# Start-up of a fused convolution and two-layer kernel: one small load on another queue, the first chunk's convolution cut by tokens, copies and w_out slots in another order

## The chip, the cores and the metric

The kernel runs on one core of a Trainium2 chip. Its time is device microseconds for one execution. Before the change, three executions took 680.83, 681.26 and 681.55 us, a median of 681.26 us. The engines are named as the profile names them: PE (TensorE matmuls), PEld (its weight loads), DVE (VectorE), ACT (ScalarE), POOL (GpSimd), SP (SyncE). SPq, ACTq and POOLq are their sequencers, which issue DMAs.

## The reference, cut to what matters

`x` is 8 x 4096 x 192 (batch, sequence, features), `weight` 8 x 7, `moe_w_in` 192 x 2048, `moe_w_out` 2048 x 192, all fp32. The output is 32768 x 192 fp32.

```python
w = exp(weight - max(weight)); w = w / (sum(w) + 1e-9)      # 8 heads x 7 taps
x_pad = 6 zero rows ahead of each sequence
y[b, s, head, :] = sum over k of w[head, k] * x_pad[b, s + k, head, :]   # 24 features a head
h = y.reshape(32768, 192) @ w_in
g = maximum(0.01 * h, h)
out = g @ w_out
```

So there are a causal convolution with seven taps, a matrix product to 2048 features, a leaky ReLU and a product back to 192.

## The kernel before, in words

**Layout.** Two sequences are worked on at a time: one in partitions 0 to 63, one in 64 to 127 (`e` = 0 and 1), and the 192 features are three chunks of 64 (`c`). So `xt` and `yt` hold features on partitions and tokens along a row. The tokens are cut into blocks of 512. A *group* (L72) is a block, except that the first two blocks are halved: groups with index 0 to 3 have T = 256 tokens (times two sequences), from index 4 on T = 512.

**The pipeline.** For each group, `mm1` (L488) multiplies `yt` with `w_in` for step `u` into the PSUM tile `ph` (two buffers), and ACT applies the leaky ReLU from `ph` into `g` (L515). For T = 256 a group has eight steps `u`, 12 matmuls each; for T = 512 sixteen steps. A loop index `j` holds two steps. The second product comes a group later in *slots*: up to index 4, `mm2_row_slot` (L533) issues two matmuls of 64x192 a slot (L525), after that `mm2_slot` (L568). How many slots follow which `j` is written out by hand in `plan` (L650); `between` (L656) says how many of them are put ahead of each of the two steps of a `j`. Sixteen slots make a round, and between the two rounds of a pair PE waits for a small ACT instruction (L555).

**The convolution.** From index 2 on it runs on DVE, as 21 taps a group (L222, L228), issued during the group before. For indices 0 and 1 most of it runs on PE: `pe_conv_jobs` (L244) multiplies `xt` with diagonal 64x64 matrices `diag` (part 0 the bf16 taps, part 1 their remainders, seven taps each) into PSUM, and an evacuation scales by `rsum` (L268). With `cross=True` each half's output goes to the opposite half of the PSUM partitions, so that two such lists, run together, use all four 64x64 quarters of the array. Group 1's chunk 1 is convolved on DVE (`conv_1`, L690) while its chunks 0 and 2 are on PE, cut into three stretches by `CUTS` (L53): after `u` = 1, 3 and 5 of group 0. Their evacuation follows `u` = 5 (L703).

**The order of the start.** Instructions go to each engine in the order of the program text (the schedule is manual), and each engine runs its own in order.

- SP issues x's first 256 tokens as two DMAs (L142); ACT issues the taps' DMA `w9` (L288), then loads its function table (L366) and computes the exponentials (L372). DVE splits them into bf16 parts `w9p` (L379 to L382).
- PE runs `warm` matmuls (L360), then `select` (L396) spreads the taps over partitions into `wps`. ACT casts x's first half (L155) and half of the second; DVE casts the rest (L155), *then* copies the taps (L409) and makes the six parts of `diag` (L420).
- PE transposes x (L181), ACT copies it to `xt` (L195), PE convolves group 0 (L259).
- `w_in` comes by POOL DMAs in bf16. Half of its rows stand in the wrong partitions for one of the sequences: `spread_up` (L326) and `spread_down` (L322) copy them across. The first half of `w_in` (`w_in[0]`) is copied in a *near* and a *far* part of 512 columns, the second (`w_in[1]`), which step `u` = 4 reads first, after that.
- Chunk 0 of group 0 is convolved as 28 matmuls of 256 columns: the bf16 part into one PSUM tile (`hi`), the remainders, crossed, into another. ACT scales the remainders into `low` (L455, two instructions), and DVE joins both to `yt` (L465). Chunks 1 and 2 follow as 56 matmuls of 256 columns.

Of the kernel before, what the change touches and what calls it, by code (L numbers as in the profile page):

```python
# [10 lines left out]
FP32 = mybir.dt.float32  # L11
# [4 lines left out]
def kernel(  # L16
# [8 lines left out]
    nc = tc.nc  # L25

    B, S, D = x.shape
    H, K = weight.shape
# [11 lines left out]
    HT = ST // 2  # L40
# [9 lines left out]
    for k in range(K):  # L50
        SKEW += [(2, k), next(pair)]
    SKEW += [(1, 5), (0, 6), (1, 6)]
    CUTS = {1: (0, 6), 3: (6, 11), 5: (11, 14)}  # L53
    GB = 32
    NR = D // (2 * GB)

    const_pool = ctx.enter_context(tc.tile_pool(name="const", bufs=1))
# [14 lines left out]
    groups = [(b, h * HT, HT) for b in range(NHALF) for h in range(2)]  # L72
# [162 lines left out]
    def y_of(grp, c):  # L235
        blk, t0, T = grp
        if blk not in yt:
            yt[blk] = yt_pool.tile([128, NCH, ST], BF16, name="yt")
        return yt[blk][:, c, t0 : t0 + T]

    def acc_tile():
        return psum_o.tile([128, ST], FP32, name="acc", tag="po")

    def pe_conv_jobs(grp, c, cross=False, parts=range(2), accs=None):  # L244

        blk, t0, T = grp
        accs = accs or [acc_tile()] * 2
        jobs = []  # L250
        for p in parts:
            for k in range(K):
                a = BASE + k + blk * ST + t0
                both = []
                for e in range(2):
                    ps = slice(e * CH, (e + 1) * CH)
                    to = slice((e ^ cross) * CH, ((e ^ cross) + 1) * CH)
                    both.append(
                        lambda k=k, p=p, a=a, ps=ps, to=to, acc=accs[e]: nc.tensor.matmul(  # L259
                            out=acc[to, :T], lhsT=diag[c][ps, p, k, :],  # L260
                            rhs=xt[0][ps, c, a : a + T],
                            start=(k == 0 and p == parts[0]),
                            stop=(k == K - 1 and p == parts[-1]),
                        )
                    )
                jobs.append(both)

        def evac(*scale, out=None):  # L268
            out = y_of(grp, c) if out is None else out
            if not cross:  # L270
                scale[0](out, accs[0][:, :T], rsum[:, c, :])
                return
            for e in range(2):
                ps = slice(e * CH, (e + 1) * CH)
                frm = slice((1 - e) * CH, (2 - e) * CH)
                scale[e](out[ps], accs[e][frm, :T], rsum[frm, c, :])

        return jobs, evac

    def run(*lists):  # L280
        for slots in zip_longest(*lists, fillvalue=()):
            for both in slots:
                for job in both:
                    job()


    w9 = const_pool.tile([H, K + 1], FP32, name="w9")
    nc.scalar.dma_start(out=w9[:, 0:K], in_=weight)  # L288
    load_first(0)

    ones = nc.const_aps.tensor(1.0, [128, ST], BF16)
# [7 lines left out]
    for sign, off in ((1, 0), (-1, GRP - 1)):  # L299
        nc.gpsimd.affine_select(  # L300
            out=sel[:, :, 0, :], in_=sel[:, :, 0, :], compare_op=mybir.AluOpType.is_ge,
# [10 lines left out]
    near, far = slice(0, WF // 2), slice(WF // 2, WF)  # L312
# [8 lines left out]
    def spread_down(n, copy=nc.vector.tensor_copy, cols=slice(0, WF)):  # L321
        copy(out=w_in[n][0:CH, 1, cols], in_=w_in[n][CH:128, 0, cols])  # L322

    def spread_up(n, slots=slice(0, 3, 2), cols=slice(0, WF)):
        to = slice(slots.start // 2 + 1, (slots.stop - 1) // 2 + 2)
        nc.vector.tensor_copy(out=w_in[n][CH:128, to, cols], in_=w_in[n][0:CH, slots, cols])  # L326
# [21 lines left out]
    for h in range(2):  # L348
        cs = slice(h * NFC // (2 * RUN), (h + 1) * NFC // (2 * RUN))
        nc.gpsimd.dma_start(  # L350
            out=w_out.rearrange("p (c i) d -> p c i d", i=RUN)[:, cs],
            in_=moe_w_out.rearrange("(c p i) d -> p c i d", p=128, i=RUN)[:, cs],
# [5 lines left out]
    def warm(n, cols=HT, to=wa[:, 0]):  # L358
# [10 lines left out]
        out=nmax, in_=w9[:, 0:K], axis=mybir.AxisListType.X,  # L369
# [3 lines left out]
        out=w9[:, 0:K], in_=w9[:, 0:K], func=mybir.ActivationFunctionType.Exp,  # L373
# [18 lines left out]
    def select(out, parts):  # L392
# [17 lines left out]
        out=taps, in_=wps_hm[..., None].to_broadcast([128, NCH, 2, K + 1, 2])  # L410
# [5 lines left out]
    def diag_wide(c, p):  # L416
# [16 lines left out]
    rsum = const_pool.tile([128, NCH, 1], FP32)  # L433
# [5 lines left out]
        out=rsum, in0=wml[:, :, K:], scalar=1e-9, in1=taps[:, :, 0, K:, 0],  # L439
        op0=mybir.AluOpType.add, op1=mybir.AluOpType.add,  # L440
# [7 lines left out]
    load_x(2)  # L448
    diag_wide(1, 1)
    diag_wide(2, 1)  # L450
    spread_up(0, slice(0, 1), near)
    spread_down(0, cols=near)

    def act_scale(out, in_, scale):
        nc.scalar.activation(  # L455
            out=out, in_=in_, func=mybir.ActivationFunctionType.Copy, scale=scale
        )

    hi = acc_tile()
    low = const_pool.tile([128, HT], FP32, name="low")  # L460
    pe_hi, _ = pe_conv_jobs(groups[0], 0, parts=(0,), accs=[hi] * 2)
    pe_lo, evac_lo = pe_conv_jobs(groups[0], 0, cross=True, parts=(1,))
    run(pe_hi, pe_lo)
    evac_lo(act_scale, act_scale, out=low)
    nc.vector.scalar_tensor_tensor(  # L465
        out=y_of(groups[0], 0), in0=hi[:, :HT], scalar=rsum[:, 0, :], in1=low,
        op0=mybir.AluOpType.mult, op1=mybir.AluOpType.add,
    )
    spread_up(0, slice(2, 3), near)
    pe_1, evac_1 = pe_conv_jobs(groups[0], 1)  # L470
    pe_2, evac_2 = pe_conv_jobs(groups[0], 2, cross=True, accs=[acc_tile(), wps[:, 0]])
# [1 line left out]
    evac_1(act_scale)  # L473
    evac_2(nc.vector.tensor_scalar_mul, act_scale)
    spread_up(0, slice(0, 1), far)
    spread_down(0, nc.scalar.copy, far)


    g, po, acc2, osb, seal = {}, {}, {}, {}, None
    NSW = 2 * NHALF  # L480
# [150 lines left out]
    def evac_o(n):  # L631
# [18 lines left out]
    plan = {  # L650
        0: [0] * 4,
        NSW - 2: [16, 8, 8, 16],
        NSW - 1: [8, 8, 16, 16],
        NSW: [16, 8, 8, 16, 8, 8, 16, 16],
    }
    between = {(1, 0): (3, 5)}  # L656
    for i, js in ((NSW - 2, (2, 3)), (NSW - 1, (1, 2)), (NSW, (2, 3, 5, 6))):
        between.update({(i, j): (0, 4) for j in js})
    slot = 0

# [9 lines left out]
    for i, grp in enumerate(groups):  # L670
        blk, t0, T = grp
        steps = T // 64
        if t0 == 0:
            g[blk] = g_pool.tile([128, NFC, 2, ST], BF16, name="g", tag="g")
        quota = plan.get(i, [16] * 4 if T == HT else [5, 5, 6, 5, 5, 6, 8, 8])

        if i == 0:
            ahead = []
        else:
            ahead = conv_jobs(groups[i + 1]) if i + 1 < len(groups) else []  # L680
        per = -(-len(ahead) // steps)
        for j in range(steps):
            early = between.get((i, j), (0, 0))
            for u in range(2 * j, 2 * j + 2):
                mm2_slots(i, early[u % 2])
                mm1(grp, u, 128 if i <= NSW else CH)
                if i == 0 and u == 0:
                    evac_first(1, nc.vector.tensor_copy, nc.vector.tensor_copy)
                    spread_up(0, slice(2, 3), far)
                    conv_1 = conv_jobs(groups[1], (1,))  # L690
                    run([conv_1[:3]])
                    spread_down(1)
                    spread_up(1, slice(0, 1), near)
                    spread_up(1, slice(2, 3))
                    run([conv_1[3:5]])
                    spread_up(1, slice(0, 1), far)
                    run([conv_1[5:]])
                    pe_0, evac_0 = pe_conv_jobs(groups[1], 0)
                    pe_2, evac_2 = pe_conv_jobs(groups[1], 2, cross=True)
                if i == 0 and u in CUTS:  # L700
                    cut = slice(*CUTS[u])
                    run(pe_0[cut], pe_2[cut])
                if i == 0 and u == 5:  # L703
                    evac_0(nc.vector.tensor_scalar_mul)
                    evac_2(nc.vector.tensor_scalar_mul, nc.vector.tensor_scalar_mul)
                if i == 0 and u == 6:
                    transpose_first(2)
                    evac_first(2, nc.vector.tensor_copy, nc.vector.tensor_copy)
            jobs = ahead[per * j : per * (j + 1)]
            if T == ST:  # L710


                jobs = ahead[len(ahead) * j // steps : len(ahead) * (j + 1) // steps]
                for job in jobs:
                    job()
                jobs = []
            mm2_slots(i, quota[j] - sum(early))
            if i == 1 and j == 1:
                load_x(3, transpose_x(2))
            for job in jobs:  # L720
                job()
            if i == 0 and j == 3:
                transpose_half(3)

            last_half = t0 + T == ST
            if i == NSW and j == steps - 1:
                evac_o(LAST - 1)
                slot = NSW * NR * NFC
            if j == steps // 4 and last_half and blk > 0:
                load_x(blk + 3)  # L730
            if j == steps // 2 and last_half and blk > 0:
                transpose_x(blk + 2)
# [35 lines left out]
```

## Time and profile before

| what | value |
|---|---|
| median of three executions | 681.26 us (680.83 to 681.55) |
| span of the profiled execution, first to last instruction | 679.2 us |
| what lies around the span, if that execution took the median | 2.1 us |
| PE busy | 674.9 us (99%) |
| ACT, DVE, POOL busy | 517.6, 481.2, 147.4 us |
| TensorE clock granted | 1.000 |

The profile has no time of its own for the whole execution apart from the span. The page's row of tenths shows PE at 9 of 10 or more in all slices but the last, where it is 8. A busy PE is not PE at its peak, so the waits and the chain have to be read as well: the chain of work that ended last is followed back from the last instruction, at each step to what released it or to the instruction before it on its engine. In the timeline, each line gives start, length, engine, line, operation, and in brackets how long the engine had been idle and what ended that.

### The profile page before, as it was taken

Reading aid. Unit: us, or ns where it says so; the run is one execution under the profiler, and the core shown is the slowest. Engines: PE = TensorE matmul, PEld = TensorE weight load, DVE = VectorE, ACT = ScalarE, POOL = GpSimd, SP = SyncE. Lnnn points to the kernel's source line nnn. Section 1 sums busy time; section 2 is a strip of 40 time slices with the busy share of each in tenths; the row PEclk is TensorE's granted clock in tenths of the full one; section 3 lists DMA queues with packets and bytes.
Section 4 is the critical chain, followed back from the end, with each engine's and each line's share of the span. In section 5 each row is a group of like instructions: output and inputs, shape, how many; then the busy total and the mean of one; then the engine's idle time right before and its main releaser. Section 6 shows DMA issues by size and latency. Waiting matters only on the chain.

```text
span 679.2 us, 27092 instructions
## 1 busy us (share of the span) xinstructions
PE 674.9 (99%) x12442; PEld 446.3 (66%) x12442; DVE 481.2 (71%) x816; ACT 517.6 (76%) x601; POOL 147.4 (22%) x208
## 2 busy tenths in 40 slices
PE   9999999999999999999999999999999999999998
PEld 6997666666666666666666666666666666666667
DVE  7989477866768766778667687667786676876612
ACT  7899877777787777777777777778777777777781
POOL 8455221122211222211222112222022220000000
PEclk9999999999999999999999999999999999999999
DMA  9999755655737656556556566567365573321123
GB/s 149 99 119 104 52 85 83 84 64 67 96 74 93 76 54 86 84 85 86 66 63 92 80 92 78 56 83 94 73 87 69 60 96 71 72 56 33 34 49 94
DMA packets 213970, 53.27 MB, mean 78 GB/s; under 512 B 209312, under 2 KB 213536, under 8 KB 213856
## 3 DMA queue, kind: packets, MB, share of 16 engines
q0 software_dynamic: 98832, 13.97, 30.3%
q1 hardware_dynamic: 115008, 37.57, 28.0%
q8 instruction: 97, 1.59, 0.9%
q14 instruction: 17, 0.14, 0.1%
q10 hardware_dynamic: 16, 0.00, 0.0%
HBM read 28.31 MB, written 25.17 MB: 79 GB/s over the span
## 4 chain that ended last, share of the span: by engine, by line
PE 98%; DVE 1%; ACT 0%; issue 0%; ACTq 0%
PE ph L507 49%; PE acc L588 44%; PE po L525 5%; PE acc L259 0%; DVE diag L420 0%; PE ptr L167 0%; ACT L366 0%; ACTq L288 0%; DVE w_in L322 0%; DVE yt L465 0%; DVE o_sb L638 0%; DVE x_half L155 0%; ACT w L372 0%; DVE w_in L326 0%; ACT junk L366 0%
## 5 line engine op out<-in xcount | busy, mean ns | idle before, releaser
L515 ACT ACTIVATE g<-ph 128x1024 bf16<-128x1024 f32 x512 | 496.6, 1021 | 139.8 <-PE ph L507 139.6
L228 DVE SCALAR_TENSOR_TENSOR yt<-xt,wk,yt 128x512 bf16<-128x512 bf16 (+1 forms) x582 | 380.1, 715 | 0.2
L507 PE MATMUL ph<-yt,w_in 64*64 64x512 bf16 (+2 forms) x6048 | 377.5, 369 | 0.3 <-DVE yt L465 0.3
L588 PE MATMUL acc<-g,w_out 64*64 64x512 bf16 x5568 | 339.9, 376 | 0.0
L507 PEld LDWEIGHTS <-w_in 64*64 64x64 bf16 (+1 forms) x6048 | 229.7, 131 | 103.4 <-issue 1.1
L588 PEld LDWEIGHTS <-w_out 64*64 64x64 bf16 x5568 | 178.2, 118 | 118.8
L96 POOL DMA_DIRECT2D x_bf<-in_x_dram x180 | 133.9, 774 | 407.6 <-DMA xt<-x_bf 405.6
L610 DVE STREAM_TRANSPOSE o_t<-acc 128x512 f32<-128x512 f32 x87 | 72.9, 875 | 182.2 <-PE acc L588 182.2
L525 PE MATMUL po<-w_out,g 64*128 64x192 bf16 (+1 forms) x640 | 36.8, 243 | 0.0
L525 PEld LDWEIGHTS <-g 64*128 64x128 bf16 (+1 forms) x640 | 32.6, 95 | 3.2 <-issue 0.4
L222 DVE TENSOR_SCALAR yt<-xt,wk 128x512 bf16<-128x512 bf16 (+1 forms) x97 | 28.8, 320 | 2.4 <-DMA xt<-x_bf 2.4
L598 ACT COPY junk<-junk 128x1 f32<-128x1 f32 x58 | 11.1, 191 | 4.1
L638 DVE COPY o_sb<-po 128x192 f32<-128x192 f32 x8 | 2.8, 356 | 6.8 <-PE po L525 3.9
L638 ACT COPY o_sb<-po 128x192 f32<-128x192 f32 x16 | 5.1, 323 | 0.3
L259 PE MATMUL acc<-xt,diag 64*64 64x256 bf16 x126 | 4.7, 272 | 0.1
L149 POOL DMA_DIRECT2D x_half<-in_x_dram x6 | 4.3, 732 | 0.9 <-DMA w_in<-in_moe_w_in_dram 0.9
L259 PEld LDWEIGHTS <-diag 64*64 64x64 bf16 x140 | 3.7, 106 | 1.0 <-issue 0.4
L360 PE MATMUL warm<-const-bfloat16-1.0 128*128 128x512 bf16 (+2 forms) x8 | 3.3, 577 | 0.8 <-PEq L752 0.8
L145 POOL DMA_DIRECT2D x_rows<-in_x_dram x4 | 2.9, 746 | 0.0
L316 POOL DMA_DIRECT2D w_in<-in_moe_w_in_dram x5 | 2.9, 593 | 0.0
L360 PEld LDWEIGHTS <-const-bfloat16-1.0 128*128 128x128 bf16 x10 | 1.2, 128 | 2.2 <-issue 2.2
L326 DVE COPY w_in<-w_in 64x512 bf16<-64x512 bf16 (+1 forms) x7 | 2.3, 337 | 0.2
(52 smaller groups left out, 25.9 us busy)
## 6 DMA issues: line engine op xcount, KB each, us to landing
out_dram<-o_t SPq DMA_DIRECT2D x112, 192.0 KB, 4.7
x_bf<-in_x_dram POOLq DMA_DIRECT2D x180, 64.0 KB, 3.1
out_dram<-o_sb SPq DMA_DIRECT2D x8, 192.0 KB, 2.8
xt<-x_bf SPq DMA_TRANSPOSE x90, 3.2
w_out<-in_moe_w_out_dram POOLq DMA_DIRECT2D x2, 384.0 KB, 8.3
out_dram<-o_t SPq DMA_DIRECT2D x8, 96.0 KB, 2.4
out_dram<-o_sb SPq DMA_DIRECT2D x8, 96.0 KB, 1.7
w_in<-in_moe_w_in_dram POOLq DMA_DIRECT2D x2, 256.0 KB, 5.5
```

Of the source, the lines that this page charges most:

```text
L96: ins = nc.gpsimd.dma_start(out=t[:, c, :, e, :], in_=src[2 * rp + e, :, :, c * CH : (c + 1) * CH],)
L222: lambda s=src, d=dst, c=c: nc.vector.tensor_scalar_mul(d, s, wk[:, c, 0:1])
L228: lambda s=src, d=dst, c=c, k=k: nc.vector.scalar_tensor_tensor(out=d, in0=s, scalar=wk[:, c, k : k + 1], in1=d, op0=mybir.AluOpType.mult, ...
L259: lambda k=k, p=p, a=a, ps=ps, to=to, acc=accs[e]: nc.tensor.matmul(out=acc[to, :T], lhsT=diag[c][ps, p, k, :], rhs=xt[0][ps, c, a : a + T ...
L360: nc.tensor.matmul(out=to[:, 0:cols], lhsT=ones[:, 0:128], rhs=ones[:, 0:cols], start=True, stop=True,)
L507: nc.tensor.matmul(out=ph[m : m + M, e, i * T : (i + 1) * T], lhsT=w_in_of(f, e, c, m, m + M), rhs=y[ps, c, t0 : t0 + T], start=(c == chun ...
L515: act = nc.scalar.activation(out=g[blk][:, nf * u : nf * (u + 1), :, t0 : t0 + T], in_=ph.rearrange("p e (i t) -> p i e t", i=nf), func=my ...
L525: return nc.tensor.matmul(out=po[m], lhsT=g[b][ps, fc, e, s * 128 : (s + 1) * 128], rhs=w_out[ps, fc, :], start=start, stop=stop,)
L588: ins = nc.tensor.matmul(out=acc2[gi, r][e * CH : (e + 1) * CH, 0:T], lhsT=w_out_of(ps, fc, r), rhs=g[b][ps, fc, e, t0 : t0 + T], start=fi ...
L598: seal = nc.scalar.copy(out=junk, in_=junk)
L610: nc.vector.transpose(out=osb[gi, 0][:, 0 : T // GB, :, r], in_=acc2.pop((gi, r))[:, 0:T].rearrange("p (j k) -> p j k", k=GB),)
L638: ins = copy(out=o_sb[:, n % 2, :], in_=po.pop(n))
```

## The change

Five edits:

1. `w9`'s DMA is issued by SP, ahead of x's two, in place of ACT.
2. Group 0's chunk 0 is convolved in two halves of 128 tokens, both parts of the taps into one PSUM tile each, the second half crossed: 56 matmuls of 128 columns. ACT evacuates them with one instruction of 128x128 and two of 64x128. `low`, its two ACT instructions and DVE's join are gone.
3. The copies of `w_in[0]`'s near part stand after these evacuations in the text (on DVE they have the same order as before). The far `spread_down` goes from ACT to DVE, ahead of the copies of group 1's transposed x.
4. On DVE, four taps of `conv_1` in place of three stand ahead of `w_in[1]`'s copies; the fifth and the sixth stand where two were before, and the last comes between the two evacuations of group 1's PE convolution. The third stretch of that convolution and its evacuation follow `u` = 4 in place of 5.
5. `plan` moves eight slots from group index 4 (the fifth; 96 to 88) to index 3 (the fourth; 48 to 56), and `between` follows.

```diff
-    CUTS = {1: (0, 6), 3: (6, 11), 5: (11, 14)}
+    CUTS = {1: (0, 6), 3: (6, 11), 4: (11, 14)}
...
-    nc.scalar.dma_start(out=w9[:, 0:K], in_=weight)
+    nc.sync.dma_start(out=w9[:, 0:K], in_=weight)
     load_first(0)
...
-    spread_up(0, slice(0, 1), near)
-    spread_down(0, cols=near)
...
-    hi = acc_tile()
-    low = const_pool.tile([128, HT], FP32, name="low")
-    pe_hi, _ = pe_conv_jobs(groups[0], 0, parts=(0,), accs=[hi] * 2)
-    pe_lo, evac_lo = pe_conv_jobs(groups[0], 0, cross=True, parts=(1,))
-    run(pe_hi, pe_lo)
-    evac_lo(act_scale, act_scale, out=low)
-    nc.vector.scalar_tensor_tensor(
-        out=y_of(groups[0], 0), in0=hi[:, :HT], scalar=rsum[:, 0, :], in1=low,
-        op0=mybir.AluOpType.mult, op1=mybir.AluOpType.add,
-    )
+    blk, t0, T = groups[0]
+    pe_a, evac_a = pe_conv_jobs((blk, t0, T // 2), 0)
+    pe_b, evac_b = pe_conv_jobs((blk, t0 + T // 2, T // 2), 0, cross=True)
+    run(pe_a, pe_b)
+    evac_a(act_scale)
+    evac_b(act_scale, act_scale)
+    spread_up(0, slice(0, 1), near)
+    spread_down(0, cols=near)
     spread_up(0, slice(2, 3), near)
...
     spread_up(0, slice(0, 1), far)
-    spread_down(0, nc.scalar.copy, far)
+    spread_down(0, cols=far)
...
-        NSW - 1: [8, 8, 16, 16],
-        NSW: [16, 8, 8, 16, 8, 8, 16, 16],
+        NSW - 1: [16, 16, 16, 8],
+        NSW: [8, 16, 8, 8, 16, 8, 8, 16],
...
-    for i, js in ((NSW - 2, (2, 3)), (NSW - 1, (1, 2)), (NSW, (2, 3, 5, 6))):
+    for i, js in ((NSW - 2, (2, 3)), (NSW, (0, 1, 3, 4, 6, 7))):
...
-                    run([conv_1[:3]])
+                    run([conv_1[:4]])
                     spread_down(1)
                     spread_up(1, slice(0, 1), near)
                     spread_up(1, slice(2, 3))
-                    run([conv_1[3:5]])
+                    run([conv_1[4:5]])
                     spread_up(1, slice(0, 1), far)
-                    run([conv_1[5:]])
+                    run([conv_1[5:6]])
...
-                if i == 0 and u == 5:
+                if i == 0 and u == 4:
                     evac_0(nc.vector.tensor_scalar_mul)
+                    run([conv_1[6:]])
                     evac_2(nc.vector.tensor_scalar_mul, nc.vector.tensor_scalar_mul)
```

## The prediction

> **What bounds the kernel.** I read the page's chain first, then the chain from 0 to 9 us, then the timelines of ACT, SP and DVE, then the stretches with their DMA share.
>
> ```profile
> ## 4 chain that ended last, share of the span: by engine, by line
> PE 98%; DVE 1%; ACT 0%; issue 0%; ACTq 0%
> ```
>
> PE holds the end, and the clock is full throughout. From 8.09 us on PE has hardly a gap: within a row of steps the last matmul of one and the first of the next start 0.08 to 0.11 us apart, as long as one matmul streams, and 0.20 where the tile shape changes. The change takes no matmul out and makes no shape change more, so it can win only PE's idle time. That is a short list: what stands ahead of the first convolution, half a microsecond ahead of 8.09, and two or three pieces of 0.1 to 0.3 up to 16 us.
>
> ```profile
> 4.00 0.32 DVE x_half L155
> 4.32 0.17 DVE taps L409
> 4.49 0.02 issue
> 4.52 0.69 DVE diag L420 x2
> ...
> 6.67 0.29 DVE w_in L326
> 6.96 0.01 issue
> 6.97 0.55 DVE w_in L322
> 7.52 0.03 issue
> 7.56 0.49 DVE yt L465
> 8.05 0.04 issue
> 8.09 0.63 PE ph L507 x8
> ```
>
> Here the chain runs through DVE: the join L465 stands behind two copies of w_in and ends at 8.04, while the last convolution matmul started at 7.485 and PE was free at 7.59. The first line matters as much: DVE's cast of x started at 3.965, and everything after it up to the taps' diagonals queues behind it.
>
> ```profile
> 0.80 0.60 ACTq L288 DMA_DIRECT2D w<-in_weight_dram  x1
> 0.81 0.96 SPq L142 DMA_DIRECT2D x_nat<-in_x_dram  x2
> 1.44 1.28 ACT L366 ACT_TABLE_LOAD   x1 [1.44 <-PEq L752]
> ...
> 3.44 0.87 ACT L155 CAST x_half<-x_nat 128x384 bf16<-128x384 f32 x2 [0.23 <-DMA x_nat<-in_x_dram]
> ```
>
> ACT stood idle for x. In the trace x's first DMA (issued at 0.81) had landed by 3.42 and the cast began at 3.445; the second (issued at 1.315) had landed by 3.94, and ACT's and DVE's casts both began at 3.965. So x, not the taps, is last at this point.
>
> ```profile
> 1.90:2.30 0.40, 0.40 (x2) 0.15 (x1) 0.35 (x2) 0.40 (x1) 0.40 (x2) 1.00 0.83 109
> 2.30:3.40 1.10, 1.10 (x4) 0.35 (x3) 0.19 (x2) 0.90 (x4) 1.02 (x4) 1.00 0.94 308
> 3.40:4.00 0.60, 0.60 (x6) 0.34 (x4) 0.53 (x7) 0.55 (x2) 0.60 (x2) 1.00 0.90 134
> ```
>
> The last two columns are the DMA engines' busy share and GB/s: they are full from 1.9 us on, first with x, then (from 3.38) with w_in.
>
> **Part 1, the taps' DMA.** ACT's table load starts up to 0.60 us earlier, and Exp, at 2.84 now, could start at about 2.4, when nmax (2.19 + 0.15) is there. Nothing uses that: `select` started at 3.676, the moment the warm matmul before it had streamed (3.356 + 0.32), and the taps' copy waits behind DVE's cast of x. On SP the new issue stands in front of both x DMAs. Its length isn't in the trace: at least 0.32 (the shortest SP issue, of o_t), at most 0.60 (this DMA on ACT), and 0.05 between two issues. I take 0.50, the step between x's own two (0.81 to 1.315); the range is 0.37 to 0.65. x lands that much later, and casts, transposes, `xt` copies and diagonals all move with it: the first convolution from 5.146 to 5.65. Loss **0.50**.
>
> **Part 2, the convolution by token halves.** Before: 28 matmuls in seven rounds of four, 5.146 to 6.054, 0.91 us with a wait of 0.11 for the second part of the diagonal. After: 14 rounds of 128 columns, the second part needed only after seven. The trace has no four such matmuls side by side. Below: 14 x 0.055 = 0.77, from x's later transposes (L167, 128 columns, two side by side every 0.055). Above: no row shows matmuls issued faster on average than 0.027 (four in 0.109 at L259, two in 0.055 at L167); 56 x 0.027 = 1.51. I take 0.85, near the lower end, since at 5.395 four of them started within 0.01 us: issue was not their limit. The saving is 0.06, the loss at worst 0.60.
> The Trainium skill ("TensorE: Matmul & The Clock Gate", section "Wait — 56ns, not 53.3ns?") speaks against this part: it says that matmuls never start less than about 25 ns apart on average, however few columns. By that rule it would take 1.40 us and the total would be worse by 0.5; the trace's four starts within 0.01 us do not show such a floor, nor do they refute it for a long row.
>
> ACT then evacuates 128 columns three times. A 256-column one takes 0.47; xt's copies of 128 and 256 columns took 0.27 and 0.38, so 0.11 less: 0.36 each. Chunk 0 is complete about 1.1 us after its matmuls, at 7.3 + 0.50, before PE has finished chunks 1 and 2 (5.146 + 0.85 + 14 x 0.109 = 7.53 + 0.50). So the 0.5 us wait for L465 goes. Late next is chunk 1's ACT evacuation, which starts 0.22 after the last matmul's start and takes 0.47, as now (7.703 to 8.177): 8.13, and its matmuls can run at 8.17 + 0.50. They ran at 8.31. So without the 0.50 PE would be 0.14 ahead; with it, it is 0.36 behind.
>
> **Parts 3 and 4, DVE's order.** On DVE L465 goes (0.51 with its gap) and the far copy L322 comes (0.58 by the near one; 0.42 was seen for one of twice the width, so 0.3 may be possible). From the diagonals' end to group 1's x copies that is +0.06: 9.28 + 0.50 against 9.22. Then a copy, the first tap and three more (to 11.68 + 0.49 + 0.50), and `w_in[1]`'s copies can start at 12.70.
>
> ```profile
> 12.21 0.42 DVE L322 COPY w_in<-w_in 64x1024 bf16<-64x1024 bf16 x1 [0.61 <-DMA w_in<-in_moe_w_in_dram]
> ...
> 13.46 0.15 PEld L507 LDWEIGHTS <-w_in 64*128 64x128 bf16 x4 [0.21 <-DVE w_in L326]
> ```
>
> Now DVE is idle there for 0.61 until `w_in[1]` lands, and PE, in step `u` = 4, waits for these copies. This sets a floor: had x not been delayed, DVE would come to them at 12.20, they would still wait for the landing (12.19, its second part 12.77), and PE would still go on at 13.46. The 0.14 would be lost there. With the delay, DVE comes at 12.70, the copy that `u` = 4 needs ends 1.20 later, and PE goes on at 13.95: **+0.49**; with the cheaper far copy +0.35. The extra tap has used up the idle time that could have absorbed the delay. After that DVE is 0.42 shorter up to its first tap for group 2 (one tap fewer behind the copies), so 17.98 against 17.92, while PE is about 0.45 later: nothing waits.
>
> **Part 5, the slots.** A slot takes 0.0825 us (16 in 1.32), eight are 0.66; the number stays, so PE's sum does. DVE's last tap for group 4 ended at 46.155, and PE first read that chunk at 46.26: the 0.10 of cover becomes about 0.8. ACT keeps up: new steps repeat the patterns at 46 to 62 us (8, then 4 + 4, then 4 + 12 slots), where PE had no gap. Cost nothing.
>
> **Sum.** +0.50 (x) and the gain of 0.14 lost at `u` = 4, less what a cheaper far copy gives: +0.35 to +0.49, I take **+0.45**. The span goes from 679.2 to 679.65. What lies around it (2.1 to the median) stays, so 681.26 becomes **681.7**.
>
> **Rivals.**
> - *A collision of x with w_in (slower).* x now runs to about 4.0 us, but w_in's first packets came at 3.38, and the engines were full. In the trace an x packet takes 0.036, a w_in packet 0.173, and an engine gets eight of these in the first transfer. If both queues take turns on an engine, its last x packets wait for 4 to 8 of w_in's: +0.7 to +1.4 more, as all 16 engines must finish. For: transposes and x loads mix packet by packet at 20 to 22 us in the trace. Against: w_in's first packets are spread over 3.38 to 3.85, and most engines are done with x by then. Total +1.1 to +1.9, about 682.8. It decides from +1.36, that is once x's second half lands after 5.3 (3.94 + 1.36).
>   The Trainium skill ("DMA: Bandwidth & Descriptors", section "Queues, rings and completion order") says that each DMA engine goes round its queues a packet at a time, of some 9 to 17 descriptors; if so, the whole of w_in's eight can stand in front of x, the upper price.
> - *The convolution is bound by issue:* 1.51 in place of 0.85 passes on as about +0.5 beside the +0.45: 682.2.
> - *x isn't late in effect* (a short issue, or the slow first packets from 1.9 to 2.3 overlap it). Then the landing of `w_in[1]` keeps its floor: 681.2, the change does nothing. For: the first 0.4 us moved only 109 GB/s.
> - *Faster.* `w_in[1]` would have to land earlier as well. All of PE's gaps after 5.15 come to about 1 us, so even 0.5 us (680.7) needs several at once.
>
> **How the numbers follow.** Forecast 681.7 (0.40); collision 682.8 (0.34); issue-bound 682.2 (0.09); floor 681.2 (0.12); faster 680.7 (0.05). 0.2%, about what a measurement here can tell from no change, is 1.36 us: slower means over 682.62, which takes most of the collision's share and little of the others (0.36); faster, under 679.9, needs more idle time than PE has to give (0.04). The range reaches from 680.9, half a measured spread under the floor, to 683.2, the collision at its upper price.
>
> **What would show it.** x's first cast at 3.9 to 4.1 and DVE's at 4.4 to 4.6 (over 5 in a collision); Exp near 2.4 with nothing earlier for it; the first convolution's 56 matmuls in 0.8 to 0.9; no DVE instruction between the convolution and the first `ph`; PE resuming `u` = 4 near 13.95, waiting for DVE; no gap at the start of group 4. It is wrong if x's cast still begins at 3.45.

## The result, and the profile after

Five executions of the changed kernel took 682.92 to 684.16 us, a median of 683.48; five of the kernel before, taken with them, a median of 681.02. The ratio is 1.0036, with a 95% interval of 1.0025 to 1.0047: slower by about 2.5 us. Taken again later (e10 below), it was 682.99 against 681.10, a ratio of 1.0030 (1.0018 to 1.0041). The forecast was 681.7, hardly a change, in a range of 680.9 to 683.2; the first time lies above that range and the second inside it.

The profiled execution took 684.16 us, with a span of 682.4. In the changed kernel's file the lines from `mm1` on stand 5 lower: `mm1`'s matmul is L502, the row slot's L520, the leaky ReLU L510, the copy of a finished row tile L633.

The page's chain, answering to the one of before, by engine:

```profile
PE 96%; ACT 2%; DMA 1%; POOL 1%; DVE 0%; issue 0%; POOLq 0%; ACTq 0%
```

PE had 98% of it. Now ACT holds 2%, and a DMA and POOL 1% each. The latter two are at the start, where the chain ends in the transfer of `w_in[1]`; this is its last part, from the chain from 0 to 16 us (start, length, what):

```profile
5.56 8.02 DMA w_in<-in_moe_w_in_dram
...
13.60 0.42 DVE w_in L322
...
14.03 0.78 DVE w_in L326 x2
...
14.86 0.62 PE ph L502 x7
```

In this execution `w_in[1]` landed at 13.57, 1.38 later than in the one of before (12.19), and step `u` = 4 resumed at 14.86. But in a second profile of the same kernel it landed at 11.54, and DVE, not the landing, decided there (e10). So these 1.4 us are that execution's, and may be why it is the slowest of the five; they are no reason for the medians.

This is DVE's timeline in that second profile (start, length, engine, line, operation):

```profile
10.96 1.53 DVE L228 SCALAR_TENSOR_TENSOR yt<-xt,wk,yt 128x256 bf16<-128x256 bf16 x3
12.52 0.42 DVE L322 COPY w_in<-w_in 64x1024 bf16<-64x1024 bf16 x1
```

DVE came to the copy as soon as its taps were done; the data had been there for 1.0.

ACT's piece is in group index 4. The chain from 44 to 69 us, a part of it:

```profile
47.61 0.66 PE po L520 x16
48.27 0.66 PE ph L502 x6
...
48.97 0.35 issue
49.33 1.94 ACT g L510 x2
51.27 0.22 ACT o_sb L633
...
51.53 0.50 PE po L520 x8
...
56.32 2.00 ACT g L510 x2
58.32 0.22 ACT o_sb L633
...
58.59 0.50 PE po L520 x8
```

Three times (51.53, 58.59, 65.64) PE takes up its slots only after two leaky ReLUs and then the small copy on ACT. The step from PE's last matmul to these slots takes 0.67, 0.73 and 0.73 us where it takes 0.21 without a wait, so 0.46, 0.52 and 0.52 are lost, 1.50 together (by the profile's modelled ends of matmuls PE is idle 0.29, 0.35 and 0.35 there). Ahead of the first, the evacuation at 49.33 began 0.35 after ACT was free, and that held a matmul up by another 0.35. In the list of waits (engine, line, what released it; then total, times and longest in us) these are the two lines:

```profile
PEld L520 <- ACT o_sb L633: 2.4, 3, 0.8
PE po L520 <- ACT o_sb L633: 1.0, 3, 0.4
```

The kernel before has no such line. Its chain in the same group runs through PE alone:

```profile
52.73 0.65 PE ph L507 x6
53.38 0.33 PE po L525 x8
53.71 0.65 PE ph L507 x6
```

### The profile page after: what moved, and what is told of

It is laid out like the page before. It is cut to its first block, busy times and chain, and to the rows that moved or that the text cites. A ratio compares the mean times of both kernels' runs of the same rounds, so it can differ in the third digit from the quotient of the medians.

```text
span 682.4 us, 27148 instructions
## 1 busy us (share of the span) xinstructions
PE 676.4 (99%) x12470; PEld 439.3 (64%) x12470; DVE 481.5 (71%) x816; ACT 517.8 (76%) x601; POOL 147.3 (22%) x208
## 3 DMA queue, kind: packets, MB, share of 16 engines
q8 instruction: 97, 1.59, 1.0%
## 4 chain that ended last, share of the span: by engine, by line
PE 96%; ACT 2%; DMA 1%; POOL 1%; DVE 0%; issue 0%; POOLq 0%; ACTq 0%
PE ph L502 47%; PE acc L583 44%; PE po L520 4%; ACT g L510 1%; DMA w_in<-in_moe_w_in_dram 1%; POOL w_in L316 0%; POOL x_rows L145 0%; DVE w_in L326 0%; POOL sel L300 0%; ACT o_sb L633 0%; PE ptr L167 0%; PE acc L259 0%; DVE w_in L322 0%; DVE o_sb L633 0%; POOL ident masks.py:199 0%
## 5 line engine op out<-in xcount | busy, mean ns | idle before, releaser
L510 ACT ACTIVATE g<-ph 128x1024 bf16<-128x1024 f32 x512 | 496.9, 1021 | 142.8 <-PE ph L502 142.3
L502 PE MATMUL ph<-yt,w_in 64*64 64x512 bf16 (+2 forms) x6048 | 377.7, 369 | 0.9 <-DVE w_in L326 0.5
L502 PEld LDWEIGHTS <-w_in 64*64 64x64 bf16 (+1 forms) x6048 | 226.3, 131 | 107.8 <-issue 1.2
L583 PEld LDWEIGHTS <-w_out 64*64 64x64 bf16 x5568 | 174.9, 118 | 122.3
L520 PE MATMUL po<-w_out,g 64*128 64x192 bf16 (+1 forms) x640 | 37.1, 243 | 1.0 <-ACT o_sb L633 1.0
L520 PEld LDWEIGHTS <-g 64*128 64x128 bf16 (+1 forms) x640 | 32.8, 95 | 5.2 <-ACT o_sb L633 2.4
L633 DVE COPY o_sb<-po 128x192 f32<-128x192 f32 x8 | 2.8, 356 | 6.8 <-PE po L520 6.8
L633 ACT COPY o_sb<-po 128x192 f32<-128x192 f32 x16 | 5.0, 320 | 0.3
L259 PE MATMUL acc<-xt,diag 64*64 64x256 bf16 (+1 forms) x154 | 5.0, 253 | 0.0
```

What stands on the lines that cost most here:

```text
L502: nc.tensor.matmul(out=ph[m : m + M, e, i * T : (i + 1) * T], lhsT=w_in_of(f, e, c, m, m + M), rhs=y[ps, c, t0 : t0 + T], start=(c == chun ...
L510: act = nc.scalar.activation(out=g[blk][:, nf * u : nf * (u + 1), :, t0 : t0 + T], in_=ph.rearrange("p e (i t) -> p i e t", i=nf), func=my ...
L520: return nc.tensor.matmul(out=po[m], lhsT=g[b][ps, fc, e, s * 128 : (s + 1) * 128], rhs=w_out[ps, fc, :], start=start, stop=stop,)
L583: ins = nc.tensor.matmul(out=acc2[gi, r][e * CH : (e + 1) * CH, 0:T], lhsT=w_out_of(ps, fc, r), rhs=g[b][ps, fc, e, t0 : t0 + T], start=fi ...
L633: ins = copy(out=o_sb[:, n % 2, :], in_=po.pop(n))
```

## The experiments

Each was timed against the kernel before on the same chip. The times are medians; "+" is the difference from the median of before that was taken with it (681.07 for e1 to e4, 680.98 for e5 to e8, 681.10 for e9 to e12, 681.11 for e13 to e15). The ratio is estimated from all executions and need not equal that of the two medians. Where the expectations name a theory S, it is that the first slot of a round's second half waits at the *seam* between the two rounds of a pair; B is the rival that moving eight slots leaves too few to cover something.

| run | what it is | median, + | ratio (95%) |
|---|---|---|---|
| e1 | the change with the old slots | 681.53, +0.46 | 1.0006 (0.9997 to 1.0015) |
| e2 | the new slots alone | 682.62, +1.55 | 1.0023 (1.0014 to 1.0032) |
| e3 | the change, taps back on ACT | 683.14, +2.07 | 1.0036 (1.0023 to 1.0048) |
| e4 | taps on SP alone | 681.33, +0.26 | 1.0006 (0.9997 to 1.0014) |
| e5 | 16 slots moved, before otherwise | 681.53, +0.55 | 1.0007 (0.9999 to 1.0016) |
| e6 | new counts, no split after a seam | 681.72, +0.74 | 1.0013 (1.0004 to 1.0021) |
| e7 | halves and DVE's order alone | 680.97, -0.01 | 1.0003 (0.9994 to 1.0012) |
| e8 | halves alone | 680.97, -0.01 | 1.0007 (0.9998 to 1.0016) |
| e9 | the change with e5's slots | 681.88, +0.78 | 1.0017 (1.0008 to 1.0026) |
| e10 | the change again | 682.99, +1.89 | 1.0030 (1.0018 to 1.0041) |
| e11 | before, one more small load on SP | 681.68, +0.58 | 1.0014 (1.0004 to 1.0025) |
| e12 | old counts, early slots put at seams | 681.70, +0.60 | 1.0009 (1.0000 to 1.0018) |
| e13 | the change, one idle ACT copy more | 682.92, +1.81 | 1.0030 (1.0018 to 1.0042) |
| e14 | slots and taps on SP | 683.33, +2.22 | 1.0033 (1.0021 to 1.0046) |
| e15 | e14, one idle ACT copy more | 682.78, +1.67 | 1.0026 (1.0016 to 1.0036) |

The profiles tell the places apart better than the medians do. Leaky ReLUs on ACT are counted here: eight in each group up to index 3, sixteen from index 4 on. Against the kernel before, the first one of index 1 shows what the start cost (it began at 18.25 there), the time from it to the first one of index 6 what the slots cost (67.82 there). What is left from there to the end of the span is the same within 0.02 in every profile but e11's.

| profiles | start, + | slots, + |
|---|---|---|
| the change, e10 | 1.39, 0.31 | 1.90, 1.90 |
| e14 | 0.21 | 1.88 |
| e2, e3, e13, e15 | -0.36, 0.87, 0.33, 0.25 | 1.58, 1.59, 1.59, 1.58 |
| e6, e12 | -0.14, 0.07 | 0.98, 0.66 |
| e5, e9 | 0.43, 0.78 | 0.26, 0.27 |
| e4 | 0.31 | 0.14 |
| e1, e7, e8, e11 | 0.26, 0.04, -0.36, 0.39 | 0.01, 0.01, 0.00, 0.00 |

In the profiles whose start is the old one (e2, e5, e6, e12) the start differs from that of before by -0.36 to +0.43, so smaller effects there can't be read from one profile; the slots repeat to 0.02. e4's 0.14 is a step between two matmuls at 46.69, just after DVE's last tap for index 4 had ended (46.63).

**Which half costs.** e1 takes the old `plan` and `between` in the changed kernel; e2 the new ones in the kernel before:

```diff
-        NSW - 1: [8, 8, 16, 16],
-        NSW: [16, 8, 8, 16, 8, 8, 16, 16],
+        NSW - 1: [16, 16, 16, 8],
+        NSW: [8, 16, 8, 8, 16, 8, 8, 16],
...
-    for i, js in ((NSW - 2, (2, 3)), (NSW - 1, (1, 2)), (NSW, (2, 3, 5, 6))):
+    for i, js in ((NSW - 2, (2, 3)), (NSW, (0, 1, 3, 4, 6, 7))):
```

e1:

> The changed kernel with the slot plan of before. Theory S (seals): the new plan lets a round end right ahead of a step with early slots, so PE waits for the ACT instruction between the rounds three times, 1.85 us in all in the changed kernel's profile; without it the time falls by 1.6 to 2.0 us, to 681.5 to 681.9, and PE has no gap from 46 to 66 us. Rival A (ACT is overloaded in group 4 whatever the plan, because the start came later and shifted it): the gaps stay, and the time falls by under 0.5 us.

e2:

> The kernel before with the new slot plan alone. Theory S: slower than before by 1.6 to 2.0 us, with the same three gaps of PE (0.8, 0.5 and 0.5 us) in group 4. Rival A (the gaps need the later start): the same as before within 0.4 us.

The start's edits cost 0.46, the slots 1.55. The interval of e1 reaches from -0.2 to +1.0 us, so its 0.46 isn't told from nothing; that of e2 is clear of it. e1 has no wait at a seam; e2, which shares nothing else with the change, has the three of them, in the same lines of the waits:

```profile
PEld L525 <- ACT o_sb L638: 2.4, 3, 0.8
PE po L525 <- ACT o_sb L638: 1.0, 3, 0.3
```

Reckoned as above, PE loses 0.46, 0.51 and 0.51 there, 1.48 together, against +1.55 measured (a little under the 1.6 to 2.0 expected).

**The taps' queue.** e3 puts the taps' DMA back on ACT in the changed kernel, e4 does the opposite in the kernel before:

```diff
-    nc.scalar.dma_start(out=w9[:, 0:K], in_=weight)
+    nc.sync.dma_start(out=w9[:, 0:K], in_=weight)
```

e3:

> The changed kernel with the taps' DMA back on ACT. Theory X (x later by 0.4 us pushes the transfers behind it together, so that w_in's second half lands 0.4 to 1.4 us later and PE's step 4 waits for it): x's first cast back at 3.45, w_in's second half lands near 12.2, time lower by 0.4 to 1.2 us. Rival Y (the late landing comes from the run, or from the new order on DVE, not from x): the landing stays anywhere from 12 to 13.6, and the time falls by less than 0.3 us.

e4:

> The kernel before with the taps' DMA on SP, nothing else. Theory X: x's first cast at 3.85, w_in's second half lands 0.4 to 1.4 us later than 12.2, time higher by 0.4 to 1.2 us. Rival Y: x's first cast at 3.85 all the same, but the landing is as before on the whole; the time rises by the 0.4 us of x at most, less what the wait for w_in's landing hides (0 to 0.4).

In the changed kernel SP issues the taps' DMA and then x's two, and ACT's cast waits for x (the timelines of SP and of ACT):

```profile
0.81 0.41 SPq L288 DMA_DIRECT2D w<-in_weight_dram  x1
1.27 0.92 SPq L142 DMA_DIRECT2D x_nat<-in_x_dram  x2
```

```profile
3.85 0.85 ACT L155 CAST x_half<-x_nat 128x384 bf16<-128x384 f32 x2 [1.10 <-DMA x_nat<-in_x_dram]
```

In e4 the casts of x began at 3.90 and 4.44, 0.46 and 0.47 later than before, for +0.26; `w_in[1]` landed at 11.76, earlier than before. So theory X, that x pushes the transfers behind it, found no support here, and the time is within what Y allowed. e3 has the early casts (3.34 and 3.93), an early landing (11.40) and the three waits, 1.49 together, yet took +2.07, 0.6 more than the waits and only 0.34 less than the change. By the table of places its profile lost 1.59 in the slots, like e2, and 0.87 in the start, which was late in another way (its first convolution began at 5.44 in spite of the early casts: see the last section). Whether all its executions had that, six times do not tell: this remainder is open.

**Where the seam falls.** A pair of row tiles has two rounds of 16 slots. When the first round ends, the text places a copy on ACT (L638: a row tile of the pair before it; for the first pair a dummy), and PE's first slot of the second round waits for that copy. Counting slots gives the phase. Up to the end of index 3 the old plan has issued 96, three whole pairs; so in index 4 the first round of a pair ends at the end of `j` = 0, 3 and 6, and `j` = 1, 4 and 7 are unsplit: two steps of `mm1` come before the next slot. The new plan has issued 104 there: half a round more. With its counts the first rounds end at the end of `j` = 0, 3 and 6 too, but `j` = 1, 4 and 7 put four slots ahead of their second step. One step (0.65 us) stands between the seam and the next slot. e5 moves a whole round, 16 slots, so that a `j` without early slots follows each seam again; e6 keeps the new counts but splits only the `j` in which the first round of a pair ends:

```diff
-        NSW - 1: [8, 8, 16, 16],
-        NSW: [16, 8, 8, 16, 8, 8, 16, 16],
+        NSW - 1: [16, 16, 16, 16],
+        NSW: [8, 8, 16, 8, 8, 16, 8, 8],
...
-    for i, js in ((NSW - 2, (2, 3)), (NSW - 1, (1, 2)), (NSW, (2, 3, 5, 6))):
+    for i, js in ((NSW - 2, (2, 3)), (NSW, (1, 2, 4, 5, 7))):
```

```diff
-        NSW - 1: [8, 8, 16, 16],
-        NSW: [16, 8, 8, 16, 8, 8, 16, 16],
+        NSW - 1: [16, 16, 16, 8],
+        NSW: [8, 16, 8, 8, 16, 8, 8, 16],
...
-    for i, js in ((NSW - 2, (2, 3)), (NSW - 1, (1, 2)), (NSW, (2, 3, 5, 6))):
+    for i, js in ((NSW - 2, (2, 3)), (NSW, (0, 3, 6))):
```

e5:

> The kernel before, with sixteen slots (a whole round) moved from group 4 to group 3 in place of eight: 64 and 80. Rounds then end again where no early slots follow within one step. Theory S (the cost of the new plan is where the rounds fall, not how many slots were moved): no gap of PE over 0.25 us in group 4, time as before within 0.3 us (680.8 to 681.4). Rival B (fewer slots leave PE too little work beside ACT in group 4): twice as many slots moved cost more than eight did, 1.55 us or more, 682.6 to 684.

e6:

> The kernel before, with the changed kernel's numbers of slots (56 and 88) but without early slots in the steps that follow the end of a half pair (loop steps 1, 4 and 7 of group 4), so that the slots that need ACT's instruction between the rounds come after two steps. Theory S: the three gaps go, time as before within 0.3 us. Rival B: ACT is behind anyway, the gaps move to the next slots or steps, and at least 1 us of the 1.55 stays.

In e5, with twice as many slots moved, the waits are gone, and the chain in group 4 runs on PE alone:

```profile
51.94 0.65 PE ph L507 x6
52.58 0.33 PE po L525 x8
52.91 0.65 PE ph L507 x6
```

So it is the phase, not the number moved: the slots' cost falls from 1.58 to 0.26 in the table of places. The median is still 0.55 up, more than the 0.3 that was expected, with an interval that just takes in zero. Part of the 0.26 is a step between two matmuls at the end of the group, at 65.4, that takes 0.36 where others take 0.21; e9 has it too (at 65.8), the kernel before has not. The other part of the median is open; in this profile the start was 0.43 late. In e6 the waits at the seam are gone as well, but ACT stays in the chain:

```profile
52.31 1.94 ACT g L515 x2
...
54.27 2.01 ACT g L515 x2
...
56.32 0.84 PE ph L507 x6
```

Here PE does both steps after the seam, but the second waits for a `ph` buffer, as ACT is still behind with its evacuations: three gaps of about 0.3, half of e2's price by the medians (+0.74), 0.98 of 1.58 by the places. That is more than theory S expected (0.3) and less than B (at least 1). So there are two causes that work together: the slot that comes one step after the seam, and ACT, which is late there.

e12 puts early slots at the seams of the *old* plan, with no count changed:

```diff
-    for i, js in ((NSW - 2, (2, 3)), (NSW - 1, (1, 2)), (NSW, (2, 3, 5, 6))):
+    for i, js in ((NSW - 2, (2, 3)), (NSW - 1, (1, 2)), (NSW, (1, 4, 7))):
```

> The kernel before with its own numbers of slots in every group; only the early slots in group 4 stand in loop steps 1, 4 and 7, which follow the end of a half pair, in place of 2, 3, 5 and 6. No slot changes its group. Theory S (PE waits where a round's ACT instruction has only one step to hide behind): three gaps of PE of about 0.5 us, slower by 1.3 to 1.9 us. Rival B (the cost of the new plan is the smaller number of slots in group 4): as before within 0.3 us.

This missed: +0.60 in place of 1.3 to 1.9. The waits for `o_sb` are there but short (0.7 on PEld for three, against 2.4). What it lost are two gaps of 0.3 later, between the two steps of `j` = 2 and of `j` = 5 (at 51.63 and 58.49), where PE waits for a `ph` buffer. Here the round ends with 16 unbroken slots (1.32 us), in which ACT catches up; in the new plan it ends four slots (0.33) after a step. So one step of cover cost little at the seam by itself; it is too little with ACT two evacuations behind.

**The start's other edits.** e7 has the conv halves and both changes of order, e8 the halves alone; both have the old slots and the taps' DMA on ACT.

e7:

> The changed kernel with the taps' DMA on ACT and the old slot plan: the convolution by halves and the new order of DVE's work alone. Theory F (the floor: PE is 0.1 to 0.4 us ahead at the first product, and loses it in step 4, which waits for w_in's second half): as before within 0.3 us. Rival G (DVE, with one more tap ahead of the copies of w_in's second half and the far copy, is last at step 4): slower by 0.3 to 0.8 us, and PE's step 4 waits for a copy that DVE began after the landing.

e8:

> The kernel before with the convolution by halves alone; DVE's later order, the far copy on ACT, the taps' DMA and the slots as before. Theory F: the first product starts up to 0.4 us earlier, the landing of w_in's second half still holds step 4: as before, at most 0.2 us faster. Rival H (56 short matmuls are bound by issue, or ACT's three evacuations are last): the first convolution takes over 1.2 us and the time rises by 0.3 us or more.

The first `ph` came at 7.66 and 7.62, against 8.09 before: the wait for L465 is gone and 0.43 to 0.47 are won there. Not all of that is the edit's: the first convolution began 0.10 and 0.19 earlier in these two profiles, and in e2, which still has L465 but ran the copies ahead of it faster, the first `ph` came at 7.76. The medians are those of before. In e7 the gain is lost at `w_in[1]`, which had landed at 11.23, while DVE came to it at 12.14, after its third tap in this line of its timeline (start, length, line, operation):

```profile
10.59 1.52 DVE L228 SCALAR_TENSOR_TENSOR yt<-xt,wk,yt 128x256 bf16<-128x256 bf16 x3
12.14 0.42 DVE L322 COPY w_in<-w_in 64x1024 bf16<-64x1024 bf16 x1
```

No bracket means that DVE waited for nothing. Group 1 began at 17.41 (17.37 before). In e8, with one tap fewer, the copies began at 11.60 as `w_in[1]` landed (11.57), and group 1 at 17.02; its span, 678.8, is 0.4 shorter. The median does not show it, and the landing differs from one execution to the next; so a gain from the halves alone is not shown.

e11 loads the taps a second time, by SP ahead of x, into a tile that nothing reads; the kernel's own load stays on ACT:

```diff
+    w9x = const_pool.tile([H, K], FP32, name="w9x")
+    nc.sync.dma_start(out=w9x, in_=weight)
     load_first(0)
```

> The kernel before with one more DMA of the same small size on SP ahead of x (the taps, into a tile that nothing reads); the taps that are used still come by ACT. Theory X (the cost of the taps' new place is x's delay alone): x's first cast at 3.8 to 3.9, time as with the taps on SP, 0.2 to 0.6 us over before. Rival Z (what costs is elsewhere, such as the earlier table load on ACT): as before within 0.15 us.

x's casts began at 3.83 and 4.31. The times are +0.26 (e4, its interval taking in zero) and +0.58 (e11). But e11 isn't x's delay alone: of the 0.82 by which its span is longer, 0.39 lie in the start and 0.43 behind the last leaky ReLU, at the end of the kernel, where no other profile differs. Why, is open. The start of the four profiles whose only edit there delays x (e4, e11, e14, e15, the last with the idle instruction below) is 0.21 to 0.39 late.

**The whole change, mended and again.** e9 is the changed kernel with e5's slots, e10 the changed kernel unaltered.

e9:

> The whole change, with sixteen slots moved in place of eight. Theory S: what is left of the change is the start alone, as with the old plan: 681.3 to 682.0, no gap of over 0.3 us in group 4. Rival B: at least as slow as the change with eight, 683 or more.

e10:

> The changed kernel once more, beside the others on one chip. Theory: 683.2 to 683.7; the three waits for ACT in group 4 are there again; the landing of w_in's second half moves from run to run, so the start of group 1 need not be as late as in the first profile (18.76), but somewhere from 17.4 to 18.8. Rival: the start of group 1 is again near 18.8, so the late landing belongs to the change and not to the run.

e9 has no wait at a seam and is 1.1 us faster than e10. e10 came out 0.2 below the range expected for it, and its `w_in[1]` landed 2.0 earlier than in the changed kernel's first profile, so the late landing does not belong to the change. e9 doesn't beat the kernel before, and no other version does.

**The pause on ACT.** The three waits make up 1.5 of the change's 2.46, and the start 0.46; some 0.5 is left (in e10, at +1.89, nothing is). In both profiles there is a pause ahead of one evacuation (0.35 at 48.97 in the chain above). In the trace it stands between a wait of ACT and the 64th instruction that is recorded on ACT: 0.355 long in the changed kernel, e10, e1 and e4, which all have the taps' DMA on SP, and 0.04 ahead of the same evacuation in e2 and e3, which have it on ACT, so that all that follows stands one place later. e13 adds one idle instruction to ACT in the changed kernel; e14 has the slots and the taps' DMA alone; e15 adds the idle instruction to e14:

```diff
         bias=nmax, scale=1.0, accum_out=w9[:, K : K + 1],
     )
+    nc.scalar.copy(out=junk, in_=junk)
```

e13:

> The whole change plus one idle ACT copy (128x1) after the taps' Exp, at a time when ACT waits for x. Theory P: the pause of 0.355 us between ACT's wait and its evacuation near the start of group index 4 belongs to a place in ACT's stream of instructions (it stood before the 64th recorded one), and the taps' DMA, taken off ACT, moved the wait to that place. With one instruction more the pause falls elsewhere, under an evacuation: 0.04 between wait and evacuation, the three waits for o_sb stay, about 0.3 us less than the change: 682.7 to 683.1. Rival: the pause comes from SP's DMA or from the new order as such; then it stays and the time with it (683.0 to 683.5).

e14:

> The kernel before with only the new slots and the taps' DMA on SP. Theory P: the pause of 0.355 appears at ACT's 64th recorded instruction, ahead of the first of the three waits; cost 1.5 for the waits, 0.3 for the pause, 0.3 for x's delay: 683.1 to 683.4, more than the two edits alone add up to (1.55 + 0.26). Rival: without the new order there is no pause, and the costs add: 682.9.

e15:

> The same with one idle ACT copy more at the start. Theory P: no pause, three waits: 682.8 to 683.0, 0.3 less than without the copy. Rival: the idle copy changes nothing.

The chain in e14, and then in e13:

```profile
47.77 0.02 ACTq L515
47.78 0.35 issue
48.14 1.94 ACT g L515 x2
```

```profile
47.90 0.02 ACTq L511
47.91 0.04 issue
47.96 1.94 ACT g L511 x2
```

One instruction more, and the pause is gone from the chain; with it goes 0.55 from e14 to e15 (all eight times of e15 but one are below all five of e14). From the changed kernel to e13 the medians differ by 0.56, from e10 by 0.07, with spreads that overlap: there the time alone would prove nothing, and the traces carry the reading: the slots cost 1.88 to 1.90 in the three profiles with the pause (the change, e10, e14), 1.58 to 1.59 in the four with the same slots and no pause (e2, e3, e13, e15). Its place in ACT's stream decides it, not SP's DMA. What the pause is, no run here shows.

## Why the prediction was wrong, point by point

- **Part 5, the slots: the step that failed.** It said that ACT keeps up because "new steps repeat the patterns at 46 to 62 us (8, then 4 + 4, then 4 + 12 slots), where PE had no gap. Cost nothing." The same counts do recur, but half a round out of step with the rounds. In the rows read for it, the 4 + 12 slots end a pair's first round and two steps without slots between them follow; in the new plan the 4 + 4 end it and the 4 + 12 follow. The wait at L555 was named in the text of the kernel and not carried into the step. It measured +1.55 (e2; 1.58 by the places) where the sum had 0; e5 shows that the phase made it, e6 and e12 that ACT's two evacuations ahead of the copy have a share.
- **Part 1, the taps' DMA: right in kind, less in size.** The predicted delay of x was 0.50 (0.37 to 0.65). The casts began at 3.85 and 4.35, 0.41 and 0.38 later, and the first convolution at 5.40, 0.26 later, where 5.65 was predicted. SP's issue took 0.41 where 0.32 to 0.60 was the bound; Exp began at 2.36, with nothing earlier for it. Not foreseen at all was that ACT's stream gets shorter by one instruction, and that this brings a pause of 0.31 net to the worst place of the new plan (e14, e15): by itself harmless, as e1 and e4 have it where PE is not waiting.
- **Part 2, the halves: right, but for a saving that did not come.** The 56 matmuls started within 0.92 us (5.404 to 6.321), where 0.85 was taken and 1.51 was the upper bound; the 28 before them had taken 0.91, so the 0.06 was not saved. The rule weighed against it, the Trainium skill's about 25 ns from one matmul to the next ("TensorE: Matmul & The Clock Gate", section "Wait — 56ns, not 53.3ns?"), would have made an estimated 1.40. Here 55 steps took 0.917 us, 17 ns each on average, one wait included: it doesn't hold for four quarters of the array side by side. The wait for L465 went, as said: the first `ph` came at 7.62 in e8, in part because its convolution began early.
- **Parts 3 and 4, DVE's order: right.** The gain was to be lost at `u` = 4, and the extra tap was to leave no idle time for the delay. e7 shows the first, e10 the second: the copies began at 12.52, where 12.70 was predicted, on a transfer that had landed at 11.54, and PE went on at 13.78 (13.95 predicted).
- **The sum without part 5:** +0.45 predicted, +0.46 measured (e1: 681.53 against 681.7). That they agree to 0.01 is luck: the interval of e1 is 1.2 us wide, and by the places the whole start cost 0.26 in e1, 0.31 in e10 and 0.33 in e13, as DVE and PE came to `w_in[1]` about 0.2 earlier than predicted. With part 5, 0.46 for the start, 1.55 for the slots and 0.31 for the pause (1.90 less 1.59) make 2.3; the two measurements of the whole change are 2.46 and 1.89, and the sum by the places is 2.2 in e10.
- **The rivals.** x landed late by the issue alone; no collision with `w_in` (DVE's cast at 4.35, not over 5). That x's delay has no effect isn't ruled out by e4's interval; e11's lies above zero, but with 0.43 of its span's 0.82 at the kernel's end. The start is late in all four profiles with that edit alone (by 0.21 to 0.39), which leans against it but lies inside the spread of starts; it isn't settled. The issue-bound convolution and the faster kernel did not come. What came was none of them: every rival stood in the first 16 us, and nothing was put beyond part 5's zero but the words "nothing".

## What to carry to other kernels

A schedule with counts has a phase: before a pattern of slots is called a repetition, count to where each handshake between engines falls in it, and what is queued ahead of the instruction that answers it. In this kernel a slot after a handshake needs as much work of PE's own before it as the other engine still has in its queue. An edit that takes an instruction out of one engine's stream shifts all that follow it, and that can decide by tenths of a microsecond far away.

## What the hardware showed that was not expected

**PE came to its full pace at different times.** Two `warm` matmuls, one of 512 columns, stand ahead of the first convolution. This is PE's timeline in the changed kernel, and then in e3 (start, length, line, operation):

```profile
5.01 0.46 PE L360 MATMUL wps<-const-bfloat16-1.0 128*128 128x512 bf16 x2
```

```profile
4.72 0.79 PE L360 MATMUL wps<-const-bfloat16-1.0 128*128 128x512 bf16 x2
```

In e3, e9, e11 and e12 the second of the two started 427 ns after the first, in e5 357, in the others 215. In the same four the last two transposes of 128 columns ahead of them started 106 or 107 ns apart, in the changed kernel 55. In e3 the rounds of the first convolution, too, started 107 ns apart up to 6.5 and 55 after that, and its 56 matmuls took 1.26 where the changed kernel's took 0.92. The trace's record of the granted clock fits: its first entry, 1.0, begins at 4.08 in the kernel before, at 4.59 in the changed one, at 5.64 in e12, 5.79 in e11, 6.18 in e9 and 6.53 in e3. The first convolution then began up to 0.4 later than the casts alone would give: in e3 at 5.44, with x cast at 3.34 and 3.93, and in e7 at 5.05, with 3.39 and 3.89. The page's clock row reads 9 in all slices and the mean is 1.000 all the same: in slices of 17 us it can't be seen. So the prediction's "the clock is full throughout" does not hold for the first 4 us.

**The landing of one DMA moved by microseconds.** `w_in[1]`'s first part landed between 10.40 (e11) and 13.57 (the changed kernel's first profile), with no order by edit. Before, 15 of its 16 completions were in by 10.36 and the last at 12.19. One profile of such a start is one draw.
